# A fused attention and FFN kernel: one transpose by DMA, one copy on ScalarE, and a new order at the hand-over

## The chip, the cores and the metric

The kernel runs on one core of a Trainium2 chip. The metric is the device time of one execution in microseconds; lower is better. The core has five engines that run side by side, each with its own queue of instructions worked off in order: TensorE (PE in the profile; its weight loads are shown as PEld), VectorE (DVE), ScalarE (ACT), GpSimd (POOL) and SyncE (SP), which here issues nearly all DMAs. Engines wait for each other on semaphores. Matmul results go to PSUM, everything else lives in SBUF.

## The reference

What is computed, with S = 2048 rows, D = 640, 32 heads of 20 columns, and an FFN width of 1536, all in bfloat16:

```python
qkv = layernorm(x) @ wqkv                       # q, k, v: 32 heads x 20
pq, pk = q @ w_phi[h], k @ w_phi[h]             # per head, 20 x 20
phi_q = concat(softmax(pq), softmax(-pq))       # over the 20 columns of a head
phi_k = concat(softmax(pk), softmax(-pk))
kv, z = phi_k^T @ v, sum_s phi_k
o = (phi_q @ kv) / (phi_q @ z + 1e-6)
h = x + o @ wo
out = h + (gelu(layernorm(h) @ w_gate) * (layernorm(h) @ w_up)) @ w_down
```

The attention is linear: kv needs all 2048 rows of K and V, and only after it can the first row of the output be made.

## The kernel before

The rows are cut into 16 tiles of 128. The kernel's order is written out by hand on every engine, in three stages.

*K/V loop (lines 494 to 534), over the 16 tiles t.* `k_tile(t)` makes the K projection (weights w_phi folded in) on TensorE into a PSUM tile `pk`, and ScalarE writes `E` = exp(pk) and exp(-pk), one sign each (L340). `v_mm(t + 3)` and `v_ev(t + 3)` make V for a later tile and copy it out of PSUM. `ln_ap(t + 6, on_act=True)` applies the layernorm of a still later tile on ScalarE (L151), and SP transposes the result by DMA into `LN1T`; in iterations listed in `late` it comes behind `k_tile` and `v_mm` on ScalarE instead of ahead of them. `k_norm(t)` divides E by its row sums (VectorE, GpSimd). In the last iteration `q_mm(j)` and `q_exp(j)` make phi_q for the first four groups `QG[j]` of (block of 512 rows, 128 columns), into `Eq[j]`: one 512-column matmul per 128-row slice of the weights, so 5 per (block, columns), and two activations (L401), one per sign. `kv_tile(i)` adds tile i to `kvp`, phi_k^T v for both signs, which lies in one PSUM tile. The tag "G" has four PSUM buffers in all, which pk, pv, pq, kvp, ab, po, tp and gu share.

*Hand-over (lines 535 to 541 and 831 to 882).* `kv_mask()` copies kvp out of PSUM with a scale and a bias (KT, L381) and transposes it in 32 x 32 blocks (KV, L383), for s = 0 and 1, all on VectorE. Then, tile by tile: `attn_a` multiplies phi_q by KV on TensorE in 40 small matmuls (L585) and copies the two halves to `AB`; `attn_b`, `b2`, `b3` make the quotient `o` on VectorE; `o` is transposed to `oT`, by SP's DMA (`attn_b3` with on_pe False) or on TensorE with a ScalarE copy (`attn_t`, L164 and L165); `attn_c` multiplies by `Wo` (L707); `attn_d` adds x; `attn_ds`, `attn_ln`, `attn_e` make the second layernorm, transposed to `LN2T`. Here tiles 0 and 1 are taken through to LN2T, and between their steps the remaining phi_q groups (`q_mm`, `q_exp` of q = 4 and on) keep TensorE busy. Groups 0 to 3 have two, two, two and one block; tile 0 needs the columns of groups 1, 2 and 3, the last of these written by `q_exp(3)`. Group 8 (q + 4) has one block only, so `q_mm(q + 4, (1,), ...)` issues nothing.

*FFN.* `gate_up` (L767, L770, L773) and `down` (L789, L791) run over tiles and slices of the width, and the attention of tiles 2 to 15 is woven in between them (L896 to L905).

The loads of `Wg`, `Wu` and `Wd` stand in SP's queue: two loads of Wg behind the K/V loop, released by a one-column GpSimd copy that writes to Wg and reads an Eq tile (L536); the last slice of Wg and all of Wu in `load_up()`, behind tile 0's `attn_b3`; Wd later. SP works its queue off in order, so a transpose that waits for `o` holds back the loads that stand behind it.

Of the kernel before, what the change touches and what calls it, by code (L numbers as in the profile page):

```python
# [10 lines left out]
ALU = mybir.AluOpType  # L11
ACTF = mybir.ActivationFunctionType
# [5 lines left out]
def kernel(  # L18
# [12 lines left out]
    nc = tc.nc  # L31
# [4 lines left out]
    Dh = 20  # L36
# [3 lines left out]
    NC = D // P  # L40
# [12 lines left out]
    QT = (15, 15, 15, 15)  # L53
# [9 lines left out]
    QH, QF = H // 4, D // 4  # L63
# [24 lines left out]
    Wg = const.tile([P, NC, FF], BF16, name="Wg")  # L88
    Wu = const.tile([P, NC, FF], BF16, name="Wu")
    KT = [const.tile([P, SL * 32], BF16, name=f"KT{s}") for s in range(2)]  # L90
    KV = [const.tile([P, SL, 32], BF16, name=f"KV{s}") for s in range(2)]
    row = const.tile([P, 3, 32], F32, name="row")
    sc = const.tile([P, 2], F32, name="sc")
    bi = const.tile([P, 2], F32, name="bi")

    Eq = [const.tile([P, len(g), 2, 512], BF16, name=f"Eq{j}") for j, g in enumerate(QG)]
# [14 lines left out]
    def gtile(name):  # L111
        return psG.tile([P, 2, 512], F32, name=name, tag="G")
# [94 lines left out]
    wg_v = B_w_gate.rearrange("(c p) n -> p c n", p=P)  # L207
    wu_v = B_w_up.rearrange("(c p) n -> p c n", p=P)
# [70 lines left out]
    def ln_ap(t, on_act=False, on_pe=False):  # L279
        ln = (ln_act if on_act else ln_dve)(p1, "1", *lnp[t])  # L280
        if on_pe:
            lnp[t] = ln
        else:
            transpose_to(LN1T[t // 4][:, :, t % 4 * P:(t % 4 + 1) * P], ln, False)
# [16 lines left out]
    def v_mm(t, us=(0, 1)):  # L301
        if 0 in us:
            pv[t] = gtile("pv")
        proj(pv[t], t, Wv, us)
# [26 lines left out]
    def k_tile(t):  # L331
        if t in pks:
            pk = pks[t]
            k_part(t, NC - 1)
        else:
            pk = gtile("pk")
            proj(pk, t, Wk2)
        Ek[t] = ev.tile([P, 2, D], BF16, name="E", bufs=10)
        for s in range(2):
            nc.scalar.activation(Ek[t][:, s, :].rearrange("p (u f) -> p u f", u=2), pk[:, :, 0:HD],  # L340
                                 ACTF.Exp, scale=((lnp[t][2], nrstd[t]) if t in CT else (1.0, -1.0))[s])
# [26 lines left out]
    def kv_tile(t):  # L368

        E = Ek[t].rearrange("p s (h f) -> p s h f", f=Dh)  # L370
        for i in range(QH):
            for r in range(4):
                h = r * QH + i
                nc.tensor.matmul(kvp[QUAD[r], :, i * Dh:(i + 1) * Dh], lhsT=vF[t % NV][:, h * VC:h * VC + 32],  # L374
                                 rhs=E[:, :, h, :], start=(i == t == 0), stop=(t == NT - 1), skip_group_check=True)

    def kv_mask():

        for s in range(2):
            dst = bass.AP(KT[s].tensor, KT[s].offset, [KT[s].ap[0], [Dh + 32, QH], [1, Dh]])  # L380
            nc.vector.tensor_scalar(dst, kvp[:, s].rearrange("p (h f) -> p h f", f=Dh), sc[:, s:s + 1], bi[:, s:s + 1],  # L381
                                    op0=ALU.mult, op1=ALU.add)
            nc.vector.transpose(KV[s].rearrange("p n j -> p (n j)"), KT[s])  # L383

    pqs = {}
# [1 line left out]
    def q_mm(j, part=(0, 1), kcs=range(NC)):  # L387

        if 0 in part and 0 in kcs:
            pqs[j] = gtile("pq")  # L390
        for i, bc in enumerate(QG[j]):
            if i not in part:
                continue
            b, c = divmod(bc, NC)
            for kc in kcs:
                nc.tensor.matmul(pqs[j][:, i, :], lhsT=Wq2[:, kc, c * P:(c + 1) * P], rhs=LN1T[b][:, kc, :],  # L396
                                 start=(kc == 0), stop=(kc == NC - 1))

    def q_exp(j, signs=(0, 1)):
        for s in signs:  # L400
            nc.scalar.activation(Eq[j][:, :, s, :], pqs[j][:, 0:len(QG[j])], ACTF.Exp, scale=(1.0, -1.0)[s])  # L401
# [62 lines left out]
    for s, j in ((0, VC + 1), (1, 0)):  # L464
        nc.gpsimd.tensor_scalar(sc[:, s:s + 1], row[:, 0, j:j + 1], -1.0, 1.0, op0=ALU.mult, op1=ALU.add)
        nc.gpsimd.tensor_scalar(bi[:, s:s + 1], row[:, 0, VC:VC + 1], 0.5e-6, row[:, 0, j:j + 1],
                                op0=ALU.mult, op1=ALU.add)
# [26 lines left out]
    for t in range(NT):  # L494
        if t == T3:
            kvp = gtile("kvp")[:, 0, 0:2 * QF].rearrange("p (s f) -> p s f", s=2)
        late = t in (1, 4)
        if 0 < t < NT - 6 and not late:
            ln_ap(t + 6, on_act=True)
        k_tile(t)  # L500
        if t == 0:
            ln_ap(6)
            nc.sync.dma_start(x_sb[3][:, 0:2, :], x_v[:, 12:14, :])
        if t in FQ:
            fold(WqT, Wq2, True, [i for i, f in enumerate(FQ) if f == t])
        for i in KVG.get(t, ()):
            kv_tile(i)
        for j in range(len(QT)):
            if t == QT[j]:
                q_mm(j)  # L510
                q_exp(j)
                for i in KVQ.get(j, ()):
                    kv_tile(i)
        if 0 < t < NT - 3:
            v_mm(t + 3)
        if late:
            ln_ap(t + 6, on_act=True)
        if t == 1:
            nc.sync.dma_start(x_sb[3][:, 2:4, :], x_v[:, 14:16, :])
        if 0 < t < NT - 3:  # L520
            v_ev(t + 3)
        for i in ST.get(t, ()):
            ln_st(i, i + 1)
        k_norm(t)
        load_T(WqT, 0, *[i for i, f in enumerate(LQ) if f == t])
        if t == 10:
            transpose_to(LN1T[0][:, :, P:2 * P], ln_a(1), False)
        if t == 13:
            ln_ap(0, on_act=True)
        if t == 8:  # L530
            for z in KT:
                nc.gpsimd.memset(z, 0.0)
        if t == 5:
            nc.sync.dma_start(Wo, wo_v)
    q = len(QT)
    nc.gpsimd.tensor_copy(Wg[:, 0, 0:1], Eq[q - 2][:, 0, 1, 0:1])  # L536
    for a, b in ((0, 2), (2, 4)):
        nc.sync.dma_start(Wg[:, a:b], wg_v[:, a:b])
    for t in range(13, NT):
        kv_tile(t)  # L540
    kv_mask()
    ev_cm.__exit__(None, None, None)
    p1_cm.__exit__(None, None, None)

# [5 lines left out]

    def load_up():

        nc.sync.dma_start(Wg[:, 4:NC], wg_v[:, 4:NC])
        nc.sync.dma_start(Wu, wu_v)

    def load_down(*fs):

# [12 lines left out]
    def bank(name):  # L570
        return psB[0].tile([P, 512], F32, name=name, tag="B")
# [76 lines left out]
    def attn_a(t, dve=0):  # L648
        attn_a_mm(t)
        AB, ab = ABs[t % 2], st[t, "ab"]  # L650
        for u in ((1, 0) if t in (4,) else (0, 1)):
            (nc.vector.tensor_copy if u >= 2 - dve else nc.scalar.copy)(
                AB[:, :, u * UH:(u + 1) * UH].rearrange("p s (r h) f -> p r s (h f)", r=2),
                ab[u][:, :, 0:2 * QH * KC].rearrange("p r (s x) -> p r s x", s=2))
        st[t] = AB
# [22 lines left out]
    def attn_b3(t, on_pe=False):  # L678
        AB, w = st[t]
        tt = p2.tile([P, 2, D], BF16, name="tt", bufs=2)  # L680
        num = bass.AP(AB.tensor, AB.offset, [AB.ap[0], [H * KC + 1, 2], [KC, H], [1, Dh]])
        nc.vector.tensor_tensor(  # L682
            tt.rearrange("p s (h f) -> p s h f", f=Dh), num,
            w[:, :, :, None].to_broadcast([P, 2, H, Dh]), ALU.mult)
        o = p2.tile([P, D], BF16, name="o", bufs=2)
        nc.vector.tensor_tensor(o, tt[:, 0], tt[:, 1], ALU.add)
        st[t] = o
        if not on_pe:
            attn_t(t, False)

    def attn_t(t, on_pe=True):
        oT = p2.tile([P, NC, P], BF16, name="oT", bufs=3)
        transpose_to(oT, st[t], on_pe)
        st[t] = oT

    def attn_c(t, between=None):

        if psB:
            po = pos = [bank("po")[:, 0:HD] for u in range(2)]
        else:  # L700
            po = gtile("po")
            pos = [po[:, u, 0:HD] for u in range(2)]
        for u in range(2):
            if u and between:
                between()
            for c in range(NC):
                nc.tensor.matmul(pos[u], lhsT=st[t][:, c, :], rhs=Wo[:, c, u * HD:(u + 1) * HD],  # L707
                                 start=(c == 0), stop=(c == NC - 1))
        st[t] = po
# [119 lines left out]


    q_mm(q, (0,))
    q_mm(q, (1,), (0, 1, 2, 3))
    attn_a(0, 1)
    q_mm(q, (1,), (4,))
    q_exp(q)
    q_mm(q + 1)
    attn_b(0, True)
    attn_b2(0, True)
    attn_b3(0)
    load_up()  # L840
    attn_a(1, 0)
    q_exp(q + 1, (0,))
    q_mm(q + 2)
    q_exp(q + 1, (1,))
# [1 line left out]
    q_mm(q + 3)  # L846
    attn_b(1, True)
    attn_b2(1, True)
    attn_b3(1, True)
    q_exp(q + 2, (1,))  # L850
    q_mm(q + 4, (0,), (0, 1))
    attn_c(0, lambda: attn_t(1))
    attn_d(0, False)
    q_exp(q + 3, (0,))
    q_mm(q + 4, (0,), (2, 3))
    attn_ds(0)
    attn_c(1)
    q_exp(q + 3, (1,))
    attn_d(1, False)
    q_mm(q + 4, (0,), (4,))  # L860
    q_mm(q + 4, (1,))
    q_exp(q + 4)

    def first():
# [72 lines left out]
```

## Time and profile before

| | us |
|---|---|
| three timed runs | 273.23, 271.43, 272.72 (median 272.72) |
| profiled execution, whole | 271.97 |
| its span | 270.2 |
| TensorE busy | 266.4 (99%) |
| VectorE / ScalarE / GpSimd busy | 175.1 / 138.8 / 100.7 |
| K/V loop, about | 17 to 67 |
| hand-over | 67 to 86 |
| FFN with the other tiles | 86 to 270 |

Views name an instruction by engine, line and op, then out<-in with shapes. In the timeline a row starts with its start and its length in us; "x10" are ten instructions merged, and what stands in brackets is the engine's idle time ahead of it and what ended it ("issue" if the profile shows no releaser). A matmul's own row is longer than its share of the engine, since matmuls are pipelined; the distance between starts says what one costs. DMA rows of SP give the time of issuing; landing comes later and is given by the view of a tile.

### The profile page before, as it was taken

What the parts mean: (1) busy time and instruction counts of PE and PEld (TensorE: products, weight loads), DVE (VectorE), ACT (ScalarE), POOL (GpSimd) and SP (SyncE); (2) the same over time, 40 slices, a digit from 0 to 9 for tenths busy, and PEclk for the clock granted to TensorE, in tenths of its full rate; (3) what the DMA queues carried; (4) which work ended last, traced back from release to release, by engine and by line L of the source; (5) the groups of instructions that cost most, each with busy time, mean ns of one, the idle gap of its engine ahead of it and who ended that gap; (6) DMA issues with size and microseconds to landing.
All of it is one profiled execution on the core that took longest, in us unless ns stands there. A gap on an engine that the chain in (4) does not pass through costs nothing.

```text
span 270.2 us, 7023 instructions
## 1 busy us (share of the span) xinstructions
PE 266.4 (99%) x2857; PEld 172.0 (64%) x2857; DVE 175.1 (65%) x347; ACT 138.8 (51%) x249; POOL 100.7 (37%) x238
## 2 busy tenths in 40 slices
PE   8999999999999999999999999999999999999995
PEld 7776777755455887788755455775555476444574
DVE  6889999997876758875466783568664322333322
ACT  5789998877789675245541356321544300322100
POOL 5448898796002335375211664014561100000000
PEclk9999999999999999999999999999999999999999
DMA  7997387210679442332301222403222101000011
GB/s 193 222 198 164 67 214 116 35 27 2 235 268 247 131 101 63 62 77 49 52 27 51 49 50 49 51 2 75 81 41 52 24 24 51 24 0 0 4 49 49
DMA packets 45264, 22.10 MB, mean 82 GB/s; under 512 B 37808, under 2 KB 43184, under 8 KB 45232
## 3 DMA queue, kind: packets, MB, share of 16 engines
q1 hardware_dynamic: 44576, 21.64, 33.4%
q8 instruction: 22, 0.36, 0.6%
q10 hardware_dynamic: 656, 0.03, 0.2%
q14 instruction: 10, 0.08, 0.1%
HBM read 10.18 MB, written 2.62 MB: 47 GB/s over the span
## 4 chain that ended last, share of the span: by engine, by line
PE 93%; DMA 3%; DVE 2%; ACT 1%; POOL 0%; SPq 0%; issue 0%
PE gu L767 39%; PE pd L789 20%; PE pq L396 8%; PE po L707 8%; PE pk L296 6%; PE pv L296 5%; DMA x_sb<-in_A_x_dram 3%; PE kvp L374 2%; PE wu L228 2%; PE ab L618 1%; PE ab L585 1%; PE tp L164 1%; DVE stats L121 1%; PE pv L312 1%; PE wa L248 1%; ACT E L340 0%
## 5 line engine op out<-in xcount | busy, mean ns | idle before, releaser
L770 ACT ACTIVATE g<-gu 128x512 bf16<-128x512 f32 (+1 forms) x60 | 30.5, 510 | 73.9 <-PE gu L767 73.0
L773 DVE TENSOR_TENSOR GT<-gu,g 128x512 bf16<-128x512 f32 (+1 forms) x60 | 34.4, 580 | 47.2 <-PE gu L767 39.2
L767 PE MATMUL gu<-LN2T,Wg 128*128 128x512 bf16 (+1 forms) x300 | 61.8, 337 | 0.1
L767 PE MATMUL gu<-LN2T,Wu 128*128 128x512 bf16 (+1 forms) x300 | 61.7, 336 | 0.0
L789 PE MATMUL pd<-Wd,GT 128*128 128x320 bf16 (+4 forms) x396 | 53.9, 295 | 0.0
L789 PEld LDWEIGHTS <-GT 128*128 128x128 bf16 x396 | 37.6, 98 | 14.5 <-DVE GT L773 0.2
L767 PEld LDWEIGHTS <-Wu 128*128 128x128 bf16 x300 | 29.3, 98 | 22.6
L767 PEld LDWEIGHTS <-Wg 128*128 128x128 bf16 x300 | 29.0, 98 | 21.3 <-issue 0.2
L296 PEld LDWEIGHTS <-LN1T 128*128 128x128 bf16 x290 | 27.9, 98 | 10.7 <-issue 0.3
L355 POOL TENSOR_TENSOR E<-E,rs 128x640 bf16<-128x640 bf16 x25 | 31.6, 1298 | 4.4 <-DVE rs L351 4.1
L791 DVE TENSOR_TENSOR y<-pd,x_sb 128x320 bf16<-128x320 f32 (+4 forms) x33 | 15.8, 480 | 23.8 <-PE pd L789 23.8
L707 PE MATMUL po<-Wo,oT 128*128 128x320 bf16 x160 | 24.5, 299 | 0.0
L296 PE MATMUL pk<-Wk,LN1T 128*128 128x320 bf16 x160 | 24.4, 299 | 0.1
L396 PE MATMUL pq<-LN1T,Wq 128*128 128x512 bf16 x100 | 22.9, 379 | 0.0
L347 DVE TENSOR_REDUCE sk<-E 128x64 f32<-128x1280 bf16 x16 | 22.9, 1430 | 0.0
L401 ACT ACTIVATE Eq<-pq 128x1024 bf16<-128x1024 f32 (+1 forms) x26 | 19.9, 831 | 2.8 <-PE pq L396 2.7
L707 PEld LDWEIGHTS <-oT 128*128 128x128 bf16 x160 | 15.6, 98 | 7.3 <-ACT oT L165 0.2
L340 ACT ACTIVATE E<-pk 128x640 bf16<-128x640 f32 x28 | 18.7, 746 | 3.0 <-PE pk L296 3.0
L296 PE MATMUL pv<-Wv,LN1T 128*128 128x320 bf16 x130 | 19.8, 299 | 0.0
L151 ACT ACTIVATE ln<-x_sb,v,rstd 128x640 bf16<-128x640 bf16 x14 | 12.9, 920 | 13.3 <-POOL v L746 13.1
L396 PEld LDWEIGHTS <-Wq 128*128 128x128 bf16 x100 | 9.4, 98 | 10.3
L682 DVE TENSOR_TENSOR tt<-AB,w 128x1280 bf16<-128x1280 f32 x10 | 15.1, 1506 | 0.4 <-POOL w L675 0.3
(120 smaller groups left out, 291.4 us busy)
## 6 DMA issues: line engine op xcount, KB each, us to landing
out_dram<-y SPq DMA_DIRECT2D x15, 160.0 KB, 1.9
x_sb<-in_A_x_dram SPq DMA_DIRECT2D x6, 320.0 KB, 3.9
Wu<-in_B_w_up_dram SPq DMA_DIRECT2D x1, 1920.0 KB, 9.3
Wg<-in_B_w_gate_dram SPq DMA_DIRECT2D x2, 768.0 KB, 5.4
Wd<-in_B_w_down_dram SPq DMA_DIRECT2D x1, 1440.0 KB, 6.7
Wo<-in_A_wo_dram SPq DMA_DIRECT2D x1, 800.0 KB, 5.0
x_sb<-in_A_x_dram SPq DMA_DIRECT2D x4, 160.0 KB, 2.7
Wv<-in_A_wqkv_dram SPq DMA_DIRECT2D x2, 320.0 KB, 4.2
```

The lines of the kernel that those rows point to most:

```text
L296: nc.tensor.matmul(ps[:, u, 0:HD], lhsT=lnT(t, c), rhs=W[:, c, u * HD:(u + 1) * HD], start=(c == 0), stop=(c == NC - 1))
L340: nc.scalar.activation(Ek[t][:, s, :].rearrange("p (u f) -> p u f", u=2), pk[:, :, 0:HD], ACTF.Exp, scale=((lnp[t][2], nrstd[t]) if t in C ...
L347: nc.vector.reduce_sum(sk, Ek[t].rearrange("p s (h f) -> p (s h) f", f=Dh), axis=AX.X)
L355: eng.tensor_tensor(e, e, rs[:, s * H:(s + 1) * H, None].to_broadcast([P, H, Dh]), ALU.mult)
L396: nc.tensor.matmul(pqs[j][:, i, :], lhsT=Wq2[:, kc, c * P:(c + 1) * P], rhs=LN1T[b][:, kc, :], start=(kc == 0), stop=(kc == NC - 1))
L401: nc.scalar.activation(Eq[j][:, :, s, :], pqs[j][:, 0:len(QG[j])], ACTF.Exp, scale=(1.0, -1.0)[s])
L707: nc.tensor.matmul(pos[u], lhsT=st[t][:, c, :], rhs=Wo[:, c, u * HD:(u + 1) * HD], start=(c == 0), stop=(c == NC - 1))
L767: nc.tensor.matmul(gu[i][:, 0:n], lhsT=W[:, c, f * P:(f + 1) * P], rhs=LN2T[b][:, c, a0:a1], start=(c == 0), stop=(c == NC - 1))
L770: nc.scalar.activation(g[:, 0:n], gu[0][:, 0:n], ACTF.Gelu_apprx_tanh)
L773: nc.vector.tensor_tensor(st[b, "g", f][:, a0:a1], gu[1][:, 0:n], g[:, 0:n], ALU.mult)
L789: nc.tensor.matmul(pd[:, 0:f1 - f0], lhsT=st[b, "g", f][:, tl * P:(tl + 1) * P], rhs=Wd[:, f, f0:f1], start=(f == 0), stop=(f == NF - 1), ...
L791: nc.vector.tensor_tensor(y[:, f0:f1], pd[:, 0:f1 - f0], x_sb[b][:, tl, f0:f1], ALU.add)
```

## The change

- `late` takes in t = 2 and 3: ScalarE applies the layernorms of tiles 8 and 9 behind `k_tile(2)` and `k_tile(3)`.
- `kv_mask`: the copy of the second sign goes to ScalarE, as an Identity activation with scale and bias; VectorE makes the first copy and both transposes. The activations of `q_exp(3)` move behind `kv_mask`.
- The GpSimd copy that releases Wg moves into the last iteration of the K/V loop and reads Eq[0]. Behind it SP issues all of Wg, in two loads, and the first two slices of Wu, before the transposes of o. The other three slices of Wu (`load_up`) move behind tile 1's transpose.
- In the hand-over `attn_a(0)` stands behind seven matmuls of group q instead of nine, `attn_a(1)` behind eight matmuls of group q + 1 instead of ten. All five matmuls of group q + 4 stand between `attn_c(0)` and `attn_c(1)`; before, two stood ahead of `attn_c(0)`, two between and one behind.
- Tile 1's `o` is transposed by SP's DMA instead of by TensorE and ScalarE.

```diff
     def kv_mask():
+        dst = [bass.AP(KT[s].tensor, KT[s].offset, [KT[s].ap[0], [Dh + 32, QH], [1, Dh]]) for s in range(2)]
+        src = [kvp[:, s].rearrange("p (h f) -> p h f", f=Dh) for s in range(2)]
+        nc.vector.tensor_scalar(dst[0], src[0], sc[:, 0:1], bi[:, 0:1], op0=ALU.mult, op1=ALU.add)
+        nc.scalar.activation(dst[1], src[1], ACTF.Identity, scale=sc[:, 1:2], bias=bi[:, 1:2])
         for s in range(2):
-            dst = bass.AP(KT[s].tensor, KT[s].offset, [KT[s].ap[0], [Dh + 32, QH], [1, Dh]])
-            nc.vector.tensor_scalar(dst, kvp[:, s].rearrange("p (h f) -> p h f", f=Dh), sc[:, s:s + 1], bi[:, s:s + 1],
-                                    op0=ALU.mult, op1=ALU.add)
             nc.vector.transpose(KV[s].rearrange("p n j -> p (n j)"), KT[s])
...
-        late = t in (1, 4)
+        late = t in (1, 2, 3, 4)
...
                 q_mm(j)
-                q_exp(j)
+                if j < len(QT) - 1:
+                    q_exp(j)
+                if j == 0:
+                    nc.gpsimd.tensor_copy(Wg[:, 0, 0:1], Eq[j][:, 0, 1, 0:1])
...
-    nc.gpsimd.tensor_copy(Wg[:, 0, 0:1], Eq[q - 2][:, 0, 1, 0:1])
-    for a, b in ((0, 2), (2, 4)):
+    for a, b in ((0, 2), (2, NC)):
         nc.sync.dma_start(Wg[:, a:b], wg_v[:, a:b])
+    nc.sync.dma_start(Wu[:, 0:2], wu_v[:, 0:2])
     for t in range(13, NT):
         kv_tile(t)
     kv_mask()
+    q_exp(q - 1)
...
     def load_up():
-        nc.sync.dma_start(Wg[:, 4:NC], wg_v[:, 4:NC])
-        nc.sync.dma_start(Wu, wu_v)
+        nc.sync.dma_start(Wu[:, 2:NC], wu_v[:, 2:NC])
...
     q_mm(q, (0,))
-    q_mm(q, (1,), (0, 1, 2, 3))
+    q_mm(q, (1,), (0, 1))
     attn_a(0, 1)
-    q_mm(q, (1,), (4,))
+    q_mm(q, (1,), (2, 3, 4))
     q_exp(q)
-    q_mm(q + 1)
+    q_mm(q + 1, (0,))
+    q_mm(q + 1, (1,), (0, 1, 2))
     attn_b(0, True)
     attn_b2(0, True)
     attn_b3(0)
-    load_up()
     attn_a(1, 0)
+    q_mm(q + 1, (1,), (3, 4))
     q_exp(q + 1, (0,))
     q_mm(q + 2)
     q_exp(q + 1, (1,))
...
     attn_b2(1, True)
-    attn_b3(1, True)
+    attn_b3(1)
+    load_up()
     q_exp(q + 2, (1,))
-    q_mm(q + 4, (0,), (0, 1))
-    attn_c(0, lambda: attn_t(1))
+    attn_c(0)
     attn_d(0, False)
     q_exp(q + 3, (0,))
-    q_mm(q + 4, (0,), (2, 3))
+    q_mm(q + 4, (0,))
+    q_mm(q + 4, (1,), (0,))
     attn_ds(0)
     attn_c(1)
     q_exp(q + 3, (1,))
     attn_d(1, False)
-    q_mm(q + 4, (0,), (4,))
-    q_mm(q + 4, (1,))
+    q_mm(q + 4, (1,), (1, 2, 3, 4))
     q_exp(q + 4)
```

In the built programs the order of the instructions on each engine differs in these places and in no others.

## The prediction

> **What bounds the kernel now.** I read the page first: the busy shares, then the chain that ended last.
>
> ```profile
> span 270.2 us, 7023 instructions
> ...
> PE 266.4 (99%) x2857; PEld 172.0 (64%) x2857; DVE 175.1 (65%) x347; ACT 138.8 (51%) x249; POOL 100.7 (37%) x238
> ...
> PEclk9999999999999999999999999999999999999999
> ...
> PE 93%; DMA 3%; DVE 2%; ACT 1%; POOL 0%; SPq 0%; issue 0%
> ```
>
> TensorE (PE) is busy 99% of the span, at full clock, and is 93% of the chain. An edit therefore counts in two ways only: matmuls that it takes off PE, and gaps that it opens or closes between PE's instructions. So I went through the timeline, PE's starts above all, for gaps and for work that starts the moment its input is there. Two gaps lie where the change acts. The first is in the K/V loop:
>
> ```profile
> 21.75 0.92 ACT L151 ACTIVATE ln<-x_sb,mr,rstd 128x640 bf16<-128x640 bf16 x1 [0.67 <-POOL mr L145]
> 22.58 1.28 ACT L340 ACTIVATE E<-pk 128x640 bf16<-128x640 f32 x2
> ...
> 23.91 1.52 PE L296 MATMUL pk<-Wk,LN1T 128*128 128x320 bf16 x10
> ```
>
> pv's ten matmuls started at 22.32 and take 0.136 each, so the next pk was due at 23.68. It started at 23.91, just behind the two E activations of tile 2 (end 23.86), whose PSUM buffer it takes. They stood behind the apply of tile 8, for which ScalarE had idled 0.67. The second is at the first gate matmul:
>
> ```profile
> 82.38 1.21 SPq L167 DMA_TRANSPOSE LN2T<-ln  x1
> ...
> 85.88 0.13 PEld L767 LDWEIGHTS <-Wg 128*128 128x128 bf16 x2 [0.18 <-issue]
> ```
>
> The tile view of LN2T gives 3.4 us to landing for this transpose (85.78), with the Wu load (75.80, 9.3 us, so 85.1) ahead of it. PE sat 0.18. The rest of the stretch runs without a gap, but in places with little to spare:
>
> ```profile
> 67.03 0.45 DVE L381 TENSOR_SCALAR KT<-kvp,sc,bi 128x160 bf16<-128x160 f32 x1 [1.30 <-PE kvp L374]
> ...
> 68.45 0.58 DVE L383 STREAM_TRANSPOSE KV<-KT 128x384 bf16<-128x384 bf16 x1
> 68.92 0.37 PEld L585 LDWEIGHTS <-Eq 32*128 32x128 bf16 x40 [0.42 <-issue]
> ...
> 73.92 1.21 SPq L167 DMA_TRANSPOSE oT<-o  x1
> ...
> 76.57 0.49 DVE L686 TENSOR_TENSOR o<-tt 128x640 bf16<-128x640 bf16 x1
> ```
>
> KV[1] is transposed at 69.03, while attn_a(0) has started at 68.92 and needs it half way through. And o of tile 1 is ready at 77.06, which leaves a DMA little time before attn_c(1) at 79.03.
>
> **The change part by part.** Times are on the clock of before; the 0.23 of part 2 shifts all that follows alike. PE goes on with 0.216 per 512-column matmul, 0.136 per 320-column one, 0.0075 per phi_q@KV one, and about 0.10 at each switch between full and 32-row matmuls (68.61 to 68.92 is 0.216 + 0.096).
>
> 1. Tile 1's five transposes leave PE. The chain has them as 0.28 (77.80 to 78.08): -0.28. ScalarE's copy of them (0.69) goes too, at no gain, since PE waits for no ScalarE result from there to the gate matmuls.
>
> 2. The applies of tiles 8 and 9 move behind the E activations. E of tile 2 then starts at 20.98, when v's eviction allows it, and ends at 22.3, before 23.68: -0.23. Tile 8's apply ends 0.4 later (23.07); its transpose took 3.2 before, so it lands at 26.3, and its matmuls come at 27.75. Tile 9: apply ends 25.67, lands about 28.3, needed 30.5. Cover gone, each late microsecond would cost one.
>
> 3. phi_q@KV of tile 0 stands after seven pq matmuls instead of nine: 68.49 instead of 68.92. The two matmuls follow behind it, so PE gains nothing; it must only find its inputs. KT[0] ends at 67.47 as before, KV[0] at 68.08. The built program lets ScalarE's KT[1] copy wait for VectorE's KT[0] copy, so it starts at 67.51. No row has this copy. From below: 0.31, ScalarE's copy of 176 PSUM columns (L634); from above: that plus 0.23, which two pointer operands add (0.92 for L151 against 0.69 for copies of 640 columns), 0.54; KT[1] has both operands and 160 columns, so 0.52. It ends at 68.03, KV[1] at 68.65 (transpose 0.58), in time. But q_exp(3) now stands behind it on ScalarE: its two activations (0.60 each, 0.48 apart, 66.86 to 67.95 before) run from 67.94 to 69.03. The built program makes the last four loads of attn_a(0) wait for the second of them. Unhindered they would be due at 68.49 + 36 x 0.0075 = 68.76; with 0.06 for the signal they go at 69.09: +0.34 (with a 0.31 copy +0.13).
>
> The diff alone would let the two KT copies run side by side: the row of before has them on one engine, and so says nothing against it. The Trainium skill (PSUM — Partial Sum Buffer, section on PSUM bank collisions) speaks against that: two engines may not read one PSUM bank on the same partitions at once, and both signs of kvp lie in one bank. The wait in the built program agrees; side by side, the sum would be without the 0.34.
>
> 4. Behind attn_a(0) ScalarE's and VectorE's copies come 0.08 earlier than before (last matmul 69.13 against 69.21), and so does all up to o of tile 1: AB copies of tile 1 (attn_a(1) at 71.72, no longer 71.80) and o at 76.98. SP issues oT(1) at 77.04. The tile view of oT: 2.4 to landing at least and in the median, 3.2 at most. With 2.4 it lands at 79.43, and 0.13 later its matmul starts (the gate matmul came 0.13 behind LN2T's landing): 79.56. PE arrives there at: q_mm(5) 69.90, q_mm(6) 72.55, q_mm(7) 74.71, attn_c(0) 76.87, q_mm(8) 78.23, attn_c(1) 79.31. Wait +0.25; from 0.1 (no lag) to 1.1 (3.2). oT(0) is issued at 73.84, lands at 76.2, and has 0.5 to spare. Behind oT(1) on SP stands the rest of Wu, 1.15 MB at 78.3; before, 2.3 MB was issued from 75.18.
>
> 5. Only 18 instead of 19 pq matmuls lie between attn_c(1) and the transposes of tile 1's second norm. Before, PE's 19 took 4.10 and the chain x_sb add, bn_stats, rstd, ln was 0.03 longer. Now PE needs 0.22 less; the chain 0.11 less, since the add (80.71, 0.16 behind po) no longer queues behind VectorE's bn_aggr: +0.11. Bounds 0 to 0.22.
>
> 6. The loads. The small GpSimd copy that releases Wg stands ahead of the last E product (63.19, 1.86): the product ends 0.2 later, at 65.25, and kv_tile(15) wants it at 66.6. Wg then goes out at 63.4 instead of 67.24, and 2.69 MB instead of 1.54 before oT(0). The first 0.77 MB took 4.7 us to land, the second landed 2.0 later: 63.4 + 4.7 + 2.5 x 2.0 = 73.1, just ahead of oT(0). At the mean rate of that row (1.54 MB in 6.6) it would be 74.9, and oT(0) would run into its tail: 0 to +0.5; I take 0, as the later loads have no start-up. The rest of Wu (1.15 MB) lands near 84, and LN2T(0), issued near 82.6, takes 2.4 to 2.6: -0.18.
>
> Sum: -0.28 - 0.23 + 0.34 + 0.25 + 0.11 + 0 - 0.18 = +0.01. The profiled execution took 271.97, 1.8 around its span of 270.2: 272.0. Its three timed runs have 271.43 to 273.23 and a median of 272.72, 0.75 above it; so on the footing of that median the sum is 272.7. I name the middle, 272.3.
>
> **The rivals.** (a) The waits of parts 3 to 5 stay small: a KT[1] copy of 0.31 (+0.13), oT(1) at +0.1, the norm's chain at +0.1: -0.36, 271.6; with none of them -0.69, 271.3. For it: each is a few tenths, built from starts that I shifted by hand. Against: the order of ScalarE makes q_exp(3) late whatever the copy takes. (b) Slower: the DMA transposes run among the weights. If oT(0) takes 3.4 (as LN2T(0) did behind Wu) it lands at 77.24, +0.50 at attn_c(0); oT(1) with 3.4 lands at 80.44, another +0.76 instead of 0.25; and if LN2T(0) stays at 3.4, no -0.18. Together +1.2: 273.2. It decides from about 2.6 us to landing on. For it: the longer stream ahead, and no row of oT among loads but the one at 73.92. Against: 73.1 is before 73.84, and nothing stands between oT(0) and oT(1).
> The Trainium skill (VectorE: DVE Perf Modes, section The three transpose paths) ranks TensorE before the DMA for one 128x128 block, 390 against 1309 ns, so it speaks for (b). The trace agrees in direction, with 0.28 on PE for five blocks against 2.4 to land.
> (c) The change doesn't do in the K/V loop what it says: another buffer is late and 0.23 stays: 272.2 by the sum.
>
> **How the numbers follow.** Forecast (a wash, between 271.5 and 272.9 with the scatter of the runs) 0.45; (a) 0.22; (b) 0.25; (c) 0.08. The range takes in (a) from 271.3 and (b) up to 273.2, and the 0.75 between execution and median on top of only part of it: 271.2 to 273.5. A change of 1%, 2.7 us, is about what a measurement of this kernel can tell from no change. All credits together are 0.7, so faster by over 1% needs a term that I don't see: 0.02. Slower by over 1% needs oT(1) or oT(0) over 5 us on the way: 0.03. Within 1%: 0.95.
>
> **What would show it.** In the changed profile: pk at 23.7 without a gap; a gap of PE inside attn_a(0), ended by ScalarE's Eq; attn_c(0) without a wait, attn_c(1) behind oT's landing by some 0.25; a gap of about 0.15 ahead of the second norm's transposes; the first gate matmul directly behind attn_a(2), at about 85.9 as before. Wrong: a transpose of oT that lands over 2.6 us after its issue, or a new wait of over 0.5 anywhere on PE.

## The result

The changed kernel is slower. Six runs take 273.81 to 274.85 us with a median of 273.96, six of the kernel before beside them have a median of 272.17; the ratio is 1.0077 (95% interval 1.0059 to 1.0096). The forecast was 272.3, at most 273.5.

The page of the changed kernel, first the span and the busy shares, then the chain that ended last:

```profile
span 273.1 us, 7020 instructions
...
PE 265.7 (97%) x2852; PEld 170.8 (63%) x2852; DVE 173.7 (64%) x346; ACT 138.7 (51%) x249; POOL 102.7 (38%) x238
...
PE 90%; SPq 3%; DMA 3%; DVE 1%; issue 1%; ACT 1%; ACTq 0%
```

TensorE is busy for 0.7 us less, and the span is 2.9 us longer: PE stands still for longer. This execution is the slowest of its six; part of its length lies in the start, which the change doesn't touch. The view of the waits says where else, for PE between 60 and 110 us:

```profile
PE po L711 <- DMA oT<-o: 1.1, 1, 1.1
PE pd L793 <- DVE GT L777: 1.0, 1, 1.0
```

Two new waits of about 1 us, each of them one stop. The first is at `attn_c(1)`, where the forecast had 0.25. Timeline of the changed kernel:

```profile
74.33 4.44 SPq L167 DMA_TRANSPOSE oT<-o  x2
77.41 1.52 PE L711 MATMUL po<-Wo,oT 128*128 128x320 bf16 x10
78.82 1.00 SPq L558 DMA_DIRECT2D Wu<-in_B_w_up_dram  x1
81.07 1.20 PEld L711 LDWEIGHTS <-oT 128*128 128x128 bf16 x10 [1.55 <-DMA oT<-o]
81.07 1.53 PE L711 MATMUL po<-Wo,oT 128*128 128x320 bf16 x10 [1.06 <-DMA oT<-o]
```

The first oT lands 2.45 us after its issue and is in time. The second is issued at 77.57 and lands at 81.02, after 3.46. Measured from start to start of its matmuls, PE loses 1.23 there.

The second wait is in no part of the prediction. It is at the first down matmul, 25 us behind the first one:

```profile
103.83 1.49 DVE L686 TENSOR_TENSOR tt<-AB,w 128x1280 bf16<-128x1280 f32 x1
105.35 0.49 DVE L690 TENSOR_TENSOR o<-tt 128x640 bf16<-128x640 bf16 x1
105.76 0.75 DVE L777 TENSOR_TENSOR GT<-gu,g 128x256 bf16<-128x256 f32 x2
106.23 2.62 PE L793 MATMUL pd<-Wd,GT 128*128 128x326 bf16 x18 [1.01 <-DVE GT L777]
```

pd's first matmul reads an early GT. What it waits for is the first of the two products at 105.76, which empties the PSUM bank that pd is to write. That bank belonged to the second-last `gu`, and VectorE comes to it only behind tile 4's `tt` and `o`. In the program before, the first pd has the same bank 0, but there its last user was the third-last `gu`, emptied long before. The four buffers of tag "G" are handed out as the program is built, so where a tile sits depends on the tiles and copies ahead of it. Two parts of the change reach into that order: tile 1's `tp` no longer takes a buffer, and the second KT copy and `q_exp(3)` stand elsewhere. From start to start the wait costs 1.17.

Where the time lies, as distances between PE's starts at marks in the timeline (us; e-numbers are the experiments below):

| | start to pk(2) | pk(2) to pk(4) | pk(4) to first gate | gate to first pd | pd to PE's end |
|---|---|---|---|---|---|
| before | 18.24 | 5.67 | 62.00 | 17.34 | 164.15 |
| changed | 18.91 | 5.43 | 63.37 | 18.52 | 164.12 |
| changed, e1 | 18.82 | 5.44 | 62.93 | 18.52 | 164.13 |
| tile 1 on TensorE, e3 | 18.48 | 5.44 | 62.28 | 17.35 | 164.14 |
| before, other bank, e8 | 18.35 | 5.62 | 61.88 | 18.52 | 164.16 |
| before, late alone, e10 | 18.62 | 5.44 | 61.88 | 17.35 | 164.12 |
| no fetch at oT, other bank, e11 | 18.59 | 5.44 | 62.44 | 17.33 | 164.12 |

The first column is 18.17 to 19.18 in the profiles whose programs agree there; it is scatter, and no reading below uses it.

### The profile page after: what moved, and what is told of

The parts are those of the page before. It is cut to its first block, busy times and chain, and to the rows that moved or that the text cites. A ratio compares the mean times of both kernels' runs of the same rounds, so it can differ in the third digit from the quotient of the medians.

```text
span 273.1 us, 7020 instructions
## 1 busy us (share of the span) xinstructions
PE 265.7 (97%) x2852; PEld 170.8 (63%) x2852; DVE 173.7 (64%) x346; ACT 138.7 (51%) x249; POOL 102.7 (38%) x238
## 4 chain that ended last, share of the span: by engine, by line
PE 90%; SPq 3%; DMA 3%; DVE 1%; issue 1%; ACT 1%; ACTq 0%
PE gu L771 37%; PE pd L793 19%; PE pk L296 8%; PE po L711 8%; PE pq L397 7%; PE pv L296 6%; SPq L203 2%; DMA WkT<-in_A_wqkv_dram 2%; PE kvp L374 2%; PE ab L622 1%; DMA oT<-o 1%; PE ab L589 1%; PE wa L248 1%; DVE tt L686 1%; ACT Eq L402 0%
## 5 line engine op out<-in xcount | busy, mean ns | idle before, releaser
L774 ACT ACTIVATE g<-gu 128x512 bf16<-128x512 f32 (+1 forms) x60 | 30.4, 510 | 73.9 <-PE gu L771 73.1
```

The costliest lines, as they stand in the source:

```text
L774: nc.scalar.activation(g[:, 0:n], gu[0][:, 0:n], ACTF.Gelu_apprx_tanh)
```

## The experiments

Theory A: the loss is these two waits. What makes oT late was open: the Wu load that SP issues right behind the transpose (C), the place itself (F), or something else that uses the DMA engines (E). Each group of four ran on one chip with its own runs of the kernel before (medians 272.18, 271.70 and 271.70). A ratio is near that of the means, not of the medians.

**e1: the changed kernel again.** No edit.

> The changed kernel once more, nothing edited, for a second profile and as the footing of this group. Theory A (two new waits on TensorE make the loss: 1.06 to 1.2 us at attn_c(1) for oT of tile 1, and 1.0 to 1.2 us at the first down matmul for its PSUM bank): about 274.0 us, 1.8 above the kernel before, and the profile shows both waits again, with oT of tile 1 landing 3.2 to 3.6 us after its issue. Theory B (the long landing was an accident of the one execution profiled): oT of tile 1 lands 2.4 to 2.6 us after its issue this time, its wait is about 0.25, and the time is still near 274.0, so 0.8 of the loss must lie elsewhere.

Median 274.16, ratio 1.0070 (1.0057 to 1.0083). Both waits are there again: oT(1) lands after 3.14, PE loses 0.91 at attn_c(1) and 1.17 at pd. So the late landing is no accident of one execution; B falls.

**e2: another PSUM bank for the first pd.**

```diff
+    nc.vector.memset(gtile("skip")[:, 0, 0:1], 0.0)
     attn_c(0)
```

> The changed kernel with one VectorE memset of one PSUM column ahead of attn_c(0), on a G tile that nothing reads. It takes a turn in the rotation of the four G buffers, as tile 1's transposes did, so that the first down matmul gets a bank that x_sb<-po has drained, not the second-last gate/up product. Theory A: the wait at the first pd goes, -1.1 us against the changed kernel, 272.9; oT's wait stays. Theory B' (the pd wait hides another one that ends at the same time, the Wd load or the product GT): pd starts no earlier, or the next instructions stall by as much, 273.8 to 274.0.

Median 273.80, ratio 1.0075 (1.0050 to 1.0099; one run of 276.18 lifts it). In its profile the pd wait is gone:

```profile
105.55 1.69 PE L793 MATMUL pd<-Wd,GT 128*128 128x326 bf16 x11
```

but oT(1) now took 4.38 to land, and attn_c(1) lost 2.15 instead of about 1.1. The time alone would have told nothing: the gain of one wait went into the other. The expected 272.9 was missed, which made the landing the main question.

**e3: tile 1's transposes back on TensorE, the rest of the change kept.**

```diff
-    attn_b3(1)
+    attn_b3(1, True)
...
-    attn_c(0)
+    attn_c(0, lambda: attn_t(1))
```

> The changed kernel with only tile 1's transposes back on TensorE (attn_b3(1, True), attn_t(1) between the halves of attn_c(0)). By its program the PSUM rotation is as before the change. Theory A: no oT wait (-1.1), no pd wait (-1.1), five transposes on PE (+0.28) and ScalarE's copy hidden: -1.9, 272.1, level with the kernel before. Theory B: oT's part of the loss is not real in a typical execution: -1.1 + 0.28 - 0.25, 272.9 to 273.0. If the loss lay in the order of the loads or in ScalarE's KT copy, over 273.4.

Median 272.33, ratio 1.0011 (1.0002 to 1.0020). Both waits are gone, and with them nearly all of the loss. Theory A stands: taking back this one part of the change is enough. What is left, 0.1 to 0.5 us, is the rest of the change.

**e4: the rest of Wu held back until oT(1) has landed.**

```diff
+    nc.gpsimd.tensor_copy(Wu[:, 2, 0:1], st[1][:, 0, 0:1])
     load_up()
```

> The changed kernel with the rest of the Wu load held back until oT of tile 1 has landed (a one-column GpSimd copy from that oT into Wu ahead of the load); the PSUM rotation and the pd wait stay. Theory C (the load that SP issues 1.25 us behind the transpose holds up its last packets for about 1 us): oT of tile 1 lands 2.4 to 2.6 us after its issue, attn_c(1) waits 0.25 at most, and the time falls by about 0.9 to 273.1, unless Wu then comes late for the gate matmuls (its last part needed at about 88.3, due near 85.5). Rival D (chance, or the reads of the transpose itself): oT of tile 1 still takes 3.2 or more, and the time stays at 274.0.

Median 274.30, ratio 1.0079 (1.0067 to 1.0091): no gain. The load went out at 81.30, and oT(1) still took 3.37. C falls. The DMA view of this stretch (77.6 to 81.1) shows what else was in the engines: of the transpose 672 packets, of any load none, and one packet of another queue.

```profile
DMA packets 673, 0.18 MB, mean 52 GB/s; under 512 B 672, under 2 KB 672, under 8 KB 672
...
q1 hardware_dynamic: 672, 0.16, 55.5%
q8 instruction: 1, 0.02, 1.7%
...
oT<-o SPq DMA_TRANSPOSE x1, 3.4
```

q8 moves instructions. Its packet has 16 KB, starts at 78.53, 0.88 behind the transpose's issue, and took 0.96 us. 21 packets of the transpose, of 256 B each, start while it runs (79.29 to 79.44) and take 0.83 to 0.97 us, to 80.29 and so 0.8 past its end; most others take 0.02. The page lists 22 such packets per execution against 5704 matmuls and weight loads on PE, one per 259, so it looks like PE's own program being fetched: its moment would depend on where PE stands in its program. The next three kernels test that with instructions alone.

**e5 and e6: 8 and 16 more warm-up matmuls at the start.** They run where PE waits for its first inputs.

```diff
-    warm(*[P] * 4)
+    warm(*[P] * 4, *[8] * 8)
```

e6 also has 8 in the first call of `warm`.

> The changed kernel with 8 more warm-up matmuls of 8 columns at the start, where TensorE waits for its first inputs anyway: 16 more PE instructions ahead of everything else, nothing else edited. Theory E (oT of tile 1 is late because a 16 KB instruction fetch runs through the DMA engines 0.5 to 1.2 us behind its issue; in five profiles transposes with no fetch near took 2.50 us in the mean, those with one 0.4 to 2.3 us behind their issue 3.1 to 4.7; 22 fetches of 16 KB for 5728 PE instructions make one per 256 of them, so PE's place in its program sets the moment): at 9.3 PE instructions per us the fetch comes 1.7 us sooner, near 76.7, ahead of this transpose's packets; oT lands 2.4 to 2.6 after its issue, the wait at attn_c(1) falls from 0.9-1.2 to 0.25 or less, the wait at the first pd stays 1.17: 273.2. Rival F (a transpose issued 3.2 us behind another, or in this place, takes over 3.1 whatever the fetch does): wait and time unchanged, 274.1.

> The same with 16 more warm-up matmuls of 8 columns, 32 PE instructions. Theory E: the fetch comes 3.4 us sooner, near 75.0, which is 0.7 behind the issue of oT of tile 0: now that one lands late, 3.1 to 3.4 instead of 2.45 after its issue, and attn_c(0) waits 0.2 to 0.5, while oT of tile 1 lands in 2.4 to 2.6 and attn_c(1) hardly waits: 273.3 to 273.5. Rival F: oT(0) stays at 2.45, oT(1) above 3.1, 274.1.

e5: median 274.27, ratio 1.0087 (1.0067 to 1.0106). The fetch went from 78.5 to 75.36, further than the 1.7 expected. It fell on the other transpose, and so did the delay:

```profile
77.57 1.20 PEld L711 LDWEIGHTS <-oT 128*128 128x128 bf16 x10 [1.25 <-DMA oT<-o]
77.57 1.53 PE L711 MATMUL po<-Wo,oT 128*128 128x320 bf16 x10 [0.76 <-DMA oT<-o]
...
80.02 1.52 PE L711 MATMUL po<-Wo,oT 128*128 128x320 bf16 x10
```

oT(0), never late so far, lands after 3.95 and attn_c(0) waits; oT(1) lands after 2.43 and attn_c(1) starts without a wait. The expected time (273.2) was missed because the delay moved instead of going. F falls, since the place that was slow is now fast with the same neighbours. e6: median 274.41, ratio 1.0089 (1.0065 to 1.0114). In its profile the fetch is at 74.31, 0.29 behind oT(0)'s issue: 3.12 to land, and oT(1) 2.42; PE loses only 0.1 ahead of each. That execution took 273.49; the six spread from 273.19 to 274.99, and what the slower ones met was not profiled.

**e7: 8 more warm-up matmuls and the other bank.** The edits of e5 and e2 together.

> 8 more warm-up matmuls and the other PSUM bank for the first pd together. Theory A with E: both waits go: 274.1 - 0.9 - 1.1 = 272.1, level with the kernel before. If the fetch is not the cause of oT's landing: 273.0 to 273.8, as with the other bank alone. If what the waits hid comes out elsewhere: over 273.

Median 272.87, ratio 1.0038 (1.0023 to 1.0052). Against e5 on the same chip it is 1.4 faster, near the 1.17 of the bank; oT(0) was struck again (4.10, PE loses 1.07), and so 272.1 was missed. Twelve runs spread from 271.87 to 273.65.

**e8: the kernel before with the bad bank alone.**

```diff
+    nc.vector.memset(gtile("skip")[:, 0, 0:1], 0.0)
     load_down((0, 9))
```

> The kernel before with one VectorE memset of one PSUM column on a G tile that nothing reads, ahead of the Wd load: it shifts the rotation of the G buffers so that the first pd takes the bank of the second-last gate/up product, which VectorE drains only behind tile 4's tt and o. Nothing else of the change. Theory A: the pd wait alone, 1.0 to 1.2 us, 273.3. Rival: the wait is covered (the product GT that pd reads, or the Wd load, ends no sooner), 272.2 as before.

Median 273.07, ratio 1.0043 (1.0028 to 1.0058), that is 0.8 to 1.6 us. In the table only the fourth column moves, by 1.18. The wait of the changed kernel is made here without the change:

```profile
103.90 0.75 DVE L773 TENSOR_TENSOR GT<-gu,g 128x256 bf16<-128x256 f32 x2
104.37 2.62 PE L789 MATMUL pd<-Wd,GT 128*128 128x326 bf16 x18 [1.01 <-DVE GT L773]
```

**e9 and e10: parts of the change on the kernel before.** e10 has `late = t in (1, 2, 3, 4)` alone; e9 adds the early release and order of the Wg and Wu loads.

> The kernel before with two parts of the change alone: the applies of tiles 8 and 9 behind the E activations (late = t in (1, 2, 3, 4)), and the early order of the W_gate and W_up loads; tile 1 stays on TensorE, KT on VectorE, and the first pd takes the same PSUM bank as before. Theory A: the 0.23 at pk(4) and the 0.18 at the first gate matmul go and nothing comes in their place: -0.4, a ratio of 0.9985. Rival: the early loads make the transpose of oT of tile 0 late (0.1 to 0.5) or the starts vary more than that: 0.999 to 1.002.

> The kernel before with only the applies of tiles 8 and 9 moved (late = t in (1, 2, 3, 4)). Theory A: the gap of 0.23 at pk(4) goes, ratio 0.999. Rival: the gap comes back at a later tile, 1.000.

e9: 271.64, ratio 1.0002 (0.9992 to 1.0013). e10: 271.72, ratio 1.0001 (0.9992 to 1.0010). The trace of e10 shows E of tile 2 ahead of the apply, and pk(4) right behind pv's ten matmuls (22.70 + 10 x 0.136):

```profile
21.43 1.29 ACT L340 ACTIVATE E<-pk 128x640 bf16<-128x640 f32 x2
22.60 0.92 ACT L151 ACTIVATE ln<-x_sb,mr,rstd 128x640 bf16<-128x640 bf16 x1
22.70 1.52 PE L296 MATMUL pv<-Wv,LN1T 128*128 128x320 bf16 x10
...
24.06 1.52 PE L296 MATMUL pk<-Wk,LN1T 128*128 128x320 bf16 x10
```

The 0.23 is gone from the second column (5.67 and 5.62 before, 5.44). The times don't show it; the interval of e10, -0.22 to +0.27 us, all but reaches it, and e9 missed the expected 0.4. The 0.18 at the first gate matmul isn't there to be gained: e8 and e10 load as before, LN2T(0) lands after 2.87 and 2.81, and the gate follows without a gap. The 3.40 that the prediction read was that one execution's; there a 16 KB instruction packet (81.56, 0.96 long) was still running when the transpose was issued at 82.38.

**e11: 24 PE instructions fewer at the start, and the other bank.**

```diff
-    warm(*[512] * 2, *[P] * 28)
+    warm(*[512] * 6, *[P] * 12)
...
+    nc.vector.memset(gtile("skip")[:, 0, 0:1], 0.0)
     attn_c(0)
```

> The changed kernel with the other PSUM bank for the first pd and 24 PE instructions fewer at the start (16 of the 28 short warm-up matmuls become 4 of 512 columns, the same TensorE time). Theory E: the instruction fetch that falls on oT of tile 1 at 78.5 comes over 1.5 us later, behind the packets of that transpose; oT of tile 0 and of tile 1 both land in 2.4 to 2.6, no wait over 0.25 at attn_c(0) or attn_c(1) and none at pd: all that is left is -0.28 - 0.23 + 0.34 + 0.14 - 0.18, a ratio of 0.999 to 1.000. Rival F (the transpose is slow in its place): ratio 1.003 to 1.006, as with the other bank alone.

The fetch went to 83.78. Of the DMA view of oT(1)'s stretch (77.3 to 79.8), with the same 672 packets as in e4:

```profile
q1 hardware_dynamic: 672, 0.16, 29.1%
...
oT<-o SPq DMA_TRANSPOSE x1, 2.4
```

and of the timeline:

```profile
77.15 1.52 PE L711 MATMUL po<-Wo,oT 128*128 128x320 bf16 x10
...
79.78 1.20 PEld L711 LDWEIGHTS <-oT 128*128 128x128 bf16 x10 [0.53 <-DMA oT<-o]
79.79 1.53 PE L711 MATMUL po<-Wo,oT 128*128 128x320 bf16 x10
```

No instruction packet, 2.44 and 2.43 to land, and from start to start attn_c(1) loses 0.20. Theory E's landing times came out. The fetch now stands 0.69 behind the issue of LN2T(0), which takes 3.25 to land (86.33); the first gate matmul starts at 86.47, only 0.04 late.

The expected ratio of 0.999 to 1.000 was missed. The time is 272.42, ratio 1.0028 (1.0016 to 1.0040): the change without its two accidents, and still no gain. Behind the start its columns sum to 0.17 more than before (-0.23 + 0.44 - 0.01 - 0.03); the time says 0.4 to 1.1. Against e10, which ran on the same chip in the time of the kernel before and has the same second column, they sum to 0.54 more, nearly all of it in the third column, and that lies inside 0.4 to 1.1. So what stays open is above all why the 0.23 of the second column shows in no time.

**e12: both KT copies back on VectorE, q_exp(3) back in the loop.**

```diff
-        nc.scalar.activation(dst[1], src[1], ACTF.Identity, scale=sc[:, 1:2], bias=bi[:, 1:2])
+        nc.vector.tensor_scalar(dst[1], src[1], sc[:, 1:2], bi[:, 1:2], op0=ALU.mult, op1=ALU.add)
...
-    q_exp(q - 1)
```

> The changed kernel with both KT copies back on VectorE and q_exp(3) back in the loop. By its program the first pd also takes a bank that x_sb<-po has drained, so the pd wait is gone too. Theory A: the gap of 0.25 inside attn_a(0) goes, attn_c(1) still waits 0.9 to 1.2 for oT of tile 1 (PE's instruction count is unchanged, so the fetch stays): ratio 1.001 to 1.003. Rival: the gap inside attn_a(0) stays or moves to KV, 1.003 to 1.005.

Median 272.60, ratio 1.0027 (1.0017 to 1.0037); the first pd waits for nothing (with this edit too its bank is one that x_sb<-po has emptied, without any `tp` coming back), oT(1) takes 3.45 with a fetch 0.55 behind its issue, and PE loses 1.22. Timeline:

```profile
67.53 1.02 DVE L384 STREAM_TRANSPOSE KV<-KT 128x384 bf16<-128x384 bf16 x2
...
68.28 0.64 PE L587 MATMUL ab<-KV,Eq 32*128 32x44 bf16 x40
```

attn_a(0)'s 40 matmuls take 0.64 here, 0.79 in the changed kernel, and 0.47 where nothing is missing (attn_a(1)). So about half of the stall comes from ScalarE's order. The other half stays: started two matmuls (0.43) sooner than in the kernel before, attn_a(0) is now ahead of KV[1], which VectorE ends at 68.55 even without the copy on ScalarE.

No run here beats the kernel before by more than its interval.

## Why the prediction was wrong, point by point

*Step 4 failed: the landing of oT(1).* It was sized at 2.4, with 3.2 as the worst case, and the wait at 0.25. The case of 2.4 is right as far as it goes: in e11, where it lands after 2.43, the loss is 0.20. But with PE's program as the change leaves it, an instruction fetch falls on this transpose in all five profiles (the changed kernel, e1, e2, e4 and e12), 0.48 to 1.18 behind its issue, and it lands after 3.14 to 4.38. Two tests called wrong in the prediction, a landing over 2.6 and a wait over 0.5, were met. The trace of before held the clue: the longest landings in it, 3.2 for oT and 3.8 for LN2T, belong to transposes issued at 201.45 and 127.98, each with an instruction packet behind it (8 KB of queue q14 at 1.96, 16 KB of q8 at 0.42). I took their spread as scatter among weights, and rival (b), which had the right sign and nearly the right place, was given the wrong cause. The Trainium skill (VectorE: DVE Perf Modes, section The three transpose paths), cited for that rival, ranks TensorE before the DMA; the runs agree, with 0.28 on PE against 2.4 to 4.4.

*A step was missing: which PSUM buffer the first pd gets.* The removed `tp` was costed as five transposes and a copy, and the moved KT copy and `q_exp(3)` by their times alone. They also change the order in which the four buffers are handed out. With both, the first pd gets a bank that is emptied late and waits 1.17, shown by e8 without the rest of the change and, by its absence, in e2, e3, e7, e11 and e12. Putting `tp` back (e3) gives a good bank, and so does putting the copies back without `tp` (e12): neither part alone accounts for the bad one. The list of banks could be read from the built program before any run.

*Step 1 (-0.28):* the transposes left PE, as said. *Step 2 (-0.23):* right in the trace, at the edge of what the times can show. *Step 3 (+0.34):* the copy was put at 0.52 and took 0.48, and the matmuls took 0.79 instead of 0.47, +0.32. Row of the changed kernel:

```profile
68.12 0.48 ACT L382 ACTIVATE KT<-kvp,bi,sc 128x160 bf16<-128x160 f32 x1 [0.60 <-DVE KT L381]
68.51 1.07 ACT L402 ACTIVATE Eq<-pq 128x512 bf16<-128x512 f32 x2
...
69.63 0.10 PEld L589 LDWEIGHTS <-Eq 32*128 32x128 bf16 x4 [0.19 <-ACT Eq L402]
```

Its cause was half right: "in time" for KV[1] was not true without ScalarE's queue either (e12). *Step 5 (+0.11):* from the start of attn_c(1) to that of the transposes it is 5.42 with 18 matmuls, 5.49 before with 19, so +0.15. *Step 6 (-0.18):* the gap is gone in the changed kernel, but it was no property of the kernel before. The loads ahead of oT(0) landed at 74.96, not at 73.1 and behind its issue at 74.33; it took 2.45 all the same, so the 0 for it came out by luck.

With the sizes of the trace the sum is -0.28 - 0.23 + 0.32 + 1.23 + 0.15 + 1.17 = +2.4, or +2.0 with e1's 0.91 (the table has +2.3 and +1.9 behind the start); the first comparison has 1.6 to 2.6.

## What to carry to other kernels

Taking a tile out of a shared pool, or moving a copy that frees one, can change which buffer every later tile gets, so look in the built program at what each first writer of a bank now waits for, far behind the edit too. A DMA transpose on the critical path needs slack for its slow case, and the slow case is to be looked up with what ran beside it, not taken as scatter. A gap that one profiled execution shows is worth its credit only if other executions of the same code have it.

## What the hardware showed

Over the 14 profiles, of the transposes of 128 x 640 values issued behind 57 us whose landing the trace gives, 200 had neither an instruction packet (from 1 us ahead of the issue to the landing) nor a packet of 640 B or more, of a load or store, beside them (from 1 us behind the issue to the landing): they land after 2.36 to 2.65 us, 2.52 in the mean. Another 47 had a 16 KB instruction packet that started 0.25 to 2.0 us behind their issue: 2.90 to 4.45, 3.72 in the mean. The two ranges don't overlap. The later in this window, the worse: 0.2 to 0.6 behind 3.24 in the mean, 0.6 to 1.2 behind 3.72, 1.2 to 2.0 behind 4.13. The 8 KB packets of q14, the other instruction queue, do less: the four that start 1.76 to 1.96 behind an issue go with 3.03 to 3.16. Loads and stores hurt far less: 59 transposes with their packets and no fetch have a mean of 2.44 and at most 2.94. The Trainium skill (DMA: Bandwidth & Descriptors, section Queues, rings and completion order) says that each DMA engine takes turns between its queues packet by packet. e5 looks like one engine held up so: of oT(0)'s 672 packets all but six were through by 75.6, and these six, two of its 32 small ones among them, start at 76.37 to 76.52, as the fetch ends (75.36 and 1.03). But in e4 21 packets stood still at once and ran on past the fetch's end, and 16 of the 47, with the fetch 1.76 to 1.98 behind, had none that stood still. The trace doesn't say on which engine a packet ran, so how a fetch holds up the rest stays open.

The fetch depends on PE's place in its program: 16 instructions more moved it by 3.1 us, 32 by 4.2, 24 fewer by 5.3 the other way. It isn't proportional, and the place doesn't set it exactly: the profiles of the kernel before and of e8, with the same PE instructions, had one at 67.66 and at 72.07. In the kernel before, e8 and e10, oT(0) (73.9 to 76.5) falls between fetches at 67.7 to 72.3 and 80.8 to 81.6, and nothing in the code keeps it so.
